# Two attention branches mixed by a gate, on one core: the same 1599 steps in another order

## The chip, the core and the metric

The kernel runs on one core of one Trainium2 chip. The metric is the time of one execution in microseconds of device time. Inside the core five engines run beside each other, each through a queue of its own: TensorE (PE in the profile, with its weight loads as PEld), VectorE (DVE), ScalarE (ACT), GpSimd (POOL) and SyncE (SP), which here only issues DMAs. Waits between engines and transfers are semaphores.

## The reference

One input `x` of 2048 tokens and 640 features goes through two attention branches of 32 heads with 20 features each; a sigmoid gate per token mixes the two outputs. Shapes are B=1, S=2048, D=640, H=32, Dh=20.

```python
def _A_ref(x, wqkv, w_phi, wo):                  # linear attention
    q, k, v = ...(x @ wqkv)...
    pq = einsum('bhsd,hdf->bhsf', q, w_phi);  pk = ... k, w_phi
    phi_q = concatenate([softmax(pq), softmax(-pq)], -1);  phi_k = ...
    kv = einsum('bhsf,bhsd->bhfd', phi_k, v);  z = einsum('bhsf->bhf', phi_k)
    num = einsum('bhqf,bhfd->bhqd', phi_q, kv)
    den = einsum('bhqf,bhf->bhq', phi_q, z)[..., None] + 1e-06
    return (num / den) ... @ wo

def _B_ref(x, wq, wk, wv, wo, beta):             # causal attention with a memory
    for s in range(4):                           # segments of 512 tokens
        p = softmax(qs ks^T * scale + causal mask);  a_dot = p vs
        pq = phi(qs);  a_mem = (pq M) / (pq z + 1e-06)      # phi(t) = t+1 or exp(t)
        o = sigmoid(beta) * a_mem + (1 - sigmoid(beta)) * a_dot
        pk = phi(ks);  M = M + pk^T vs;  z = z + sum(pk)
    return o ... @ wo

g = sigmoid((x * gate_w).sum(-1, keepdims=True))
return g * _A_ref(x, ...) + (1 - g) * _B_ref(x, ...)
```

## The kernel before

The tokens are cut into 16 chunks of 128 and 4 segments of 512, the heads into 8 groups of four. A function for every part of the computation takes an index and a step number; a step issues the instructions of one engine (or one DMA) for one piece of the work. One string, `ORDER`, lists all 1599 steps in the order in which they are issued. Its words are read by this loop:

```python
for word in "".join(ORDER).split():
    i = done.get(word[:2], 0)
    done[word[:2]] = i + 1
    at = word[2:]
    STEPS[word[0]](WHICH.get(word[:2], int)(i), int(word[1]), int(at) if at.isdigit() else None,
                   sca.copy if at == "a" else vec.tensor_copy)
```

A word is a letter (which function), a digit (which step) and, where there is one, a third character: a digit names the slot of PSUM that the step's tile takes, an `a` has the result copied out of PSUM by ScalarE instead of VectorE. The index is a count: the third `P0` in the list is score batch 2. All instructions go through the class `Kept`, which keeps them in program order, so each engine's queue has the list's order and no engine overtakes inside it. That is also why every instruction in the profile has line 117, the line of that class.

The steps, by letter:

- `T` turns the first 512 tokens on TensorE (`tp_ps`), `L` loads the other three segments turned. `w` are matmuls on zeros. `k`, `v`, `q` project keys, values and queries of the second branch (`proj`, `q_ps`); `K` makes key features, `k2` and `q2` bring keys and queries to the layout for the scores by DMA (`kTs`, `qTp`).
- `F` and `W` fold `w_phi` into the weights of the first branch (`fold_ps`); `D` loads the query weight turned. `A` makes that branch's key features (`k_ps`, two exponentials `Ek`, their sum, its reciprocal, the product `phk`), `B` its values and the gate's logits (`v_ps`, `vA`), `S` and `s` the sums `z`, `X` the products `KV`.
- `f` makes the first branch's query features for a segment: one matmul `pf_ps`, then two exponentials `ET` on ScalarE (`f1`, `f2`). `d` has the denominators, `n` the numerators: `n0` and `n1` matmuls (`num_ps`), `n2` and `n3` multiply on VectorE (`t`), `n4` adds on GpSimd (`oA`).
- `P` are the scores of the second branch, in 80 batches: `P0` writes row-tiled matmuls into `st_ps`, `P1` is one exponential of 128x2048 on ScalarE (`PT`), `P3` puts zeros above the diagonal on GpSimd. From batch 3 on, `st_ps` is one tile of four PSUM banks with one buffer (`banks4`).
- `U` has the attended values of a head group: `U0` column-tiled matmuls (`uv_ps`), `U1` a copy `uT`, `U2` a transposing DMA `uN`, `U3` a reciprocal on VectorE, `U4` and `U5` on GpSimd. The last four groups go through `V` instead, with no transposition (`nd_ps`).
- `Y` makes query features, `M` reads and updates the memory (`mem_ps`, `Mbd`). `l` turns finished rows by DMA (`oT`), `o` is the output projection (`o_ps`, a copy `osb`, a store). `R` loads the two output weights.
- The last four chunks of rows end in the tail: `t` turns the rows of the first branch in one DMA (into a tile that is named `phik`), `b` those of the second branch in three (into one named `kTs`); `p`, `a`, `e`, `z` are the products with the output weights, `h` copies and stores. `p0` of chunks 1 and 2 uses the four banks of the scores (`banks4("o2_ps")`).

The other four PSUM banks go by slot: a tile takes the slot that its word names, and the first write into it waits until the tile that was there has been read.

Of the kernel before, what the change touches and what calls it, by code (L numbers as in the profile page):

```python
# [15 lines left out]
def kernel(  # L16
# [800 lines left out]
    def tail_out(j, step, at, ev):  # L817
# [18 lines left out]


    ORDER = (
# [60 lines left out]

    done = {}  # L900
    for word in "".join(ORDER).split():
# [35 lines left out]
```

## Time and profile before

| what | us |
| --- | --- |
| three runs | 291.45, 291.5, 294.0 |
| median | 291.5 |
| profiled execution | 292.36 |
| its span in the profile | 290.6 |
| TensorE busy | 278.1 |
| VectorE busy | 239.8 |
| ScalarE busy | 239.6 |
| GpSimd busy | 183.8 |

The span runs from the first to the last instruction of the profiled execution; 292.36 − 290.6 = 1.8 us of its time lie outside. The granted clock of TensorE was 1.00. In a view of an engine's order of time, a line has start, duration, engine, line, operation, output and inputs by name, and in brackets the engine's idle time before it with what ended that. Durations of matmuls overlap the next one's, so a step's cost on TensorE is read from the distance of starts.

### The profile page before, as it was taken

The numbers are of one execution on the slowest core, as the hardware profiler recorded it, in microseconds if no ns is written. First come the engines' busy times: TensorE is split into PE (matmuls) and PEld (weight loads), VectorE is DVE, ScalarE is ACT, GpSimd is POOL, SyncE is SP. The second block draws the span as 40 slices with busy tenths as digits, with TensorE's granted clock in tenths as the row PEclk, the third lists the DMA queues.
The fourth block names the chain that finished last, engine by engine and source line by source line (L and its number), as shares of the span: only waits on it lengthen the run. The fifth ranks groups of instructions, "written<-read, shape, count | busy, mean of one in ns | idle before, by whom it ended". The sixth has DMA issues, their size and how long they took to land.

```text
span 290.6 us, 8207 instructions
## 1 busy us (share of the span) xinstructions
PE 278.1 (96%) x3233; PEld 176.2 (61%) x3233; DVE 239.8 (83%) x576; ACT 239.6 (82%) x260; POOL 183.8 (63%) x305
## 2 busy tenths in 40 slices
PE   8999999999999999999999999999999999898994
PEld 4676666667677546565546556556555555566673
DVE  5969999999699539999889988798898769989613
ACT  2478976998867899999999988999899998888801
POOL 8050000037346846797996899989789996998610
PEclk9999999999999999999999999999999999999999
DMA  7999960100110694546243425141736114356422
GB/s 226 252 237 215 166 142 11 36 2 20 20 20 20 203 158 89 72 86 134 39 92 72 106 58 104 39 106 36 124 72 139 26 41 111 83 122 126 106 62 90
DMA packets 79591, 28.10 MB, mean 97 GB/s; under 512 B 69952, under 2 KB 79552, under 8 KB 79552
## 3 DMA queue, kind: packets, MB, share of 16 engines
q1 hardware_dynamic: 78608, 26.84, 45.3%
q10 hardware_dynamic: 944, 0.74, 0.8%
q8 instruction: 25, 0.41, 0.6%
q14 instruction: 14, 0.11, 0.1%
HBM read 5.61 MB, written 2.62 MB: 28 GB/s over the span
## 4 chain that ended last, share of the span: by engine, by line
PE 66%; ACT 18%; DMA 5%; DVE 4%; POOL 3%; issue 3%; DVEq 0%; ACTq 0%; SPq 0%; POOLq 0%
ACT PT L117 15%; PE o_ps L117 9%; PE proj L117 8%; PE v_ps L117 8%; PE k_ps L117 8%; PE st_ps L117 7%; PE pf_ps L117 6%; PE q_ps L117 6%; PE uv_ps L117 4%; PE kv_ps L117 4%; DMA phk<-in_A_wqkv_dram 3%; PE mem_ps L117 2%; PE num_ps L117 2%; ACT ET L117 2%; PE zb_ps L117 1%
## 5 line engine op out<-in xcount | busy, mean ns | idle before, releaser
L117 ACT ACTIVATE PT<-st_ps 128x2048 bf16<-128x2048 f32 (+1 forms) x83 | 151.2, 1826 | 18.5 <-PE st_ps L117 14.0
L117 POOL TENSOR_SCALAR_AFFINE_SELECT PT<-PT 128x512 bf16<-128x512 bf16 (+2 forms) x116 | 80.5, 708 | 37.7 <-ACT PT L117 37.2
L117 PEld LDWEIGHTS <-xT 128*128 128x128 bf16 x640 | 59.5, 98 | 28.4 <-issue 5.7
L117 PE MATMUL st_ps<-qTp,kTs 32*128 32x384 bf16 (+3 forms) x512 | 31.8, 300 | 5.0 <-ACT PT L117 4.7
L117 ACT ACTIVATE Ek<-k_ps 128x640 bf16<-128x640 f32 x32 | 26.2, 893 | 6.2 <-PE k_ps L117 4.3
L117 POOL TENSOR_TENSOR Msb<-Msb,mtmp 128x84 f32<-128x84 f32 x24 | 9.3, 386 | 33.9 <-DVE mtmp L117 33.7
L117 DVE TENSOR_TENSOR t<-num_ps,dd 128x320 f32<-128x320 f32 x64 | 28.0, 481 | 2.3 <-POOL oA L117 1.3
L117 POOL TENSOR_TENSOR oA<-t,t 128x320 bf16<-128x320 f32 x32 | 29.1, 914 | 0.9 <-DVE t L117 0.7
L117 PEld LDWEIGHTS <-oT 128*128 128x128 bf16 x240 | 22.2, 98 | 10.4 <-issue 2.2
L117 PEld LDWEIGHTS <-kTs 32*128 32x128 bf16 (+1 forms) x552 | 14.8, 92 | 20.3 <-issue 16.3
L117 PE MATMUL proj<-WvB,xT 128*128 128x320 bf16 x160 | 26.2, 300 | 0.2 <-ACT vB L117 0.2
L117 PE MATMUL proj<-WkB,xT 128*128 128x320 bf16 x160 | 25.9, 300 | 0.0
L117 PE MATMUL q_ps<-xT,WqB 128*128 128x512 bf16 x100 | 24.9, 380 | 0.0
L117 PE MATMUL pf_ps<-xT,WqA 128*128 128x512 bf16 x100 | 24.9, 379 | 0.0
L117 PE MATMUL v_ps<-WvA,xT 128*128 128x320 bf16 (+1 forms) x160 | 24.5, 300 | 0.0
L117 PE MATMUL k_ps<-qTp,xT 128*128 128x320 bf16 x160 | 23.7, 299 | 0.1
L117 DVE TENSOR_REDUCE ksum<-Ek 128x64 f32<-128x1280 bf16 x16 | 23.3, 1455 | 0.0
L117 ACT ACTIVATE ET<-pf_ps 128x512 bf16<-128x512 f32 x40 | 22.0, 627 | 0.0
L117 POOL TENSOR_TENSOR oB<-td,tm 128x320 bf16<-128x320 f32 (+4 forms) x25 | 20.8, 835 | 0.4
L117 PE MATMUL o_ps<-WoA,oT 128*128 128x320 bf16 x120 | 20.3, 300 | 0.3 <-DVE tm L117 0.3
L117 PE MATMUL uv_ps<-PT,vB 128*32 128x512 bf16 (+1 forms) x448 | 20.4, 302 | 0.1
L117 PEld LDWEIGHTS <-phk 128*128 128x128 bf16 x370 | 17.6, 98 | 4.4 <-DMA phk<-in_A_x_dram 1.7
(115 smaller groups left out, 490.0 us busy)
## 6 DMA issues: line engine op xcount, KB each, us to landing
out_dram<-osb SPq DMA_DIRECT2D x12, 160.0 KB
qTp<-qd SPq DMA_DIRECT2D x8, 128.0 KB
WvB<-in_B_wv_dram SPq DMA_DIRECT2D x1, 800.0 KB
vA<-in_B_wq_dram SPq DMA_DIRECT2D x1, 800.0 KB
WvA<-in_A_wqkv_dram SPq DMA_DIRECT2D x1, 800.0 KB
WoA<-in_A_wo_dram SPq DMA_DIRECT2D x1, 800.0 KB
WoB<-in_B_wo_dram SPq DMA_DIRECT2D x1, 800.0 KB
qTp<-qd SPq DMA_DIRECT2D x8, 96.0 KB
```

The costliest lines, as they stand in the source:

```text
L117: return lambda *a, **k: kept(f(*a, **k))
```

## The change

Only the string `ORDER` is changed. The new list has the same 1599 words by letter, step and index; what differs is their order, the PSUM slots they name, and some of the `a` marks. Copies by ScalarE before and after are: `B` 23 and 22, `q` 8 and 7, `v` 4 and 5, `U` 3 and 4, `T` 0 and 1, `o` 8 and 4, `h` 2 and 4; `F` and `W` stay at 12. The first and the last lines of the diff:

```diff
-        "T00 w0 T1 T01 T02 T1 T1 T03 k00 T1 k01 k1 k02 I0 k03 k1 k00 k1 k1 K0 k01 K1 k1 K0 k02 K2 "
-        "K1 v03 k1 K2 K0 k00 k1 v1a K1 v01 k1 K2 F00 K0 L0 F01 K1 v1 v02 F1a K2 F2a v03 F1 F2 v1a "
-        "F00 v1 v00 F1a F2a F01 r0 r1 v1 v01 F1 D0 F00 F2 v02 r0 v1 F1a v03 F2a v1 r1 J4 A01 r0 "
...
-        "n10 o1 n2 P00 M02 n3 P1 n03 P3 n11 b0 M2 V00 n2 n3 M3 n4 V4 M4 Y0 Y1 P00 n4 o03 V1 P1 Y2 "
-        "P3 t0 V2 o1 Y0 V3 P3 P00 M01 Y1 P1 o02 M5 M2 Y2 o2 M3 P3 o1a P00 M4 M03 P1 V00 M2 M3 V4 "
-        "p02 V1 p11 V2 V3 P3 P00 o00 P1 M5 a0 M4 b0 o1a P3 V03 o2 V4 p00 V1 V2 V3 p01 M5 a0 b0 "
-        "p00 p13 e0 a0 e0 e0 z0 z1 z0 h0 z1 a0 h1 h0a h1 h2 h2 z0 z1 e0 h0 z0 h1 z1 h0 h2 h1a h2 ")
+        "T00 w0 T1 k01 T02 k1 T03 T1 T00 T1 k01 I1 I2 T1a I3 I4 k1 k02 I0 k03 k1 k00 k1 K0 k01 K1 "
+        "k1 K0 K2 k02 K1 k1 v03 K2 K0 v00 k1 K1 v1a v01 K2 v1a v02 v1 F00 v1 F01 L0 F1a v03 F1 "
+        "F2a F2 F00 v1 v00 F1a F2a F01 v1 F00 F1 v01 r0 F1a F2 F2a k02 r1 v1 D0 A01 r0 k1 K0 K1 "
...
+        "P3 n3 V3 n4 M4 Y0 Y1 P00 M5 o1 t0 o01 P1 Y2 P3 M02 o1 Y0 M2 P3 P00 Y1 p00 P1 p13 o2 M3 "
+        "V01 Y2 M4 V4 P3 V1 P00 V2 M02 P1 V3 a0 M2 M5 M3 p00 P3 b0 M4 V01 V4 a0 V1 V2 V3 M5 p01 "
+        "b0 e0 a0 p02 p11 z0 z1 e0 h0a h1 e0 z0 z1 h2 a0 h0a h1 h2 z0 z1 e0 h0a h1 z0 z1 h2 h0a "
+        "h1 h2 ")
```

In words: at the start, the first key projection stands between the turnings of `x`; before the first fold `F0` there are seven key and four value projections (`k0`, `v0`), where the old list has eight and two. Before the first score batch stand all 16 matmul steps of `A` and 24 of `B`, in the old list 14 and 18. In the middle the same kinds of steps are dealt out otherwise between the batches. In the tail, `p0` of chunk 1 follows the last score batch after `M0` and `a0` of chunk 0, where the old list has an output projection, `a0`, the last group's `V0` and `V4` before it.

107 rows, old and new, of the table ORDER are left out of this document.

## The prediction

> **What bounds the kernel now.** I read the page's head first, then the stretches between marks of the scores, then TensorE's own order of time, and last the waits.
>
> ```profile
> span 290.6 us, 8207 instructions
> PE 278.1 (96%) x3233; PEld 176.2 (61%) x3233; DVE 239.8 (83%) x576; ACT 239.6 (82%) x260; POOL 183.8 (63%) x305
> PE 66%; ACT 18%; DMA 5%; DVE 4%; POOL 3%; issue 3%; DVEq 0%; ACTq 0%; SPq 0%; POOLq 0%
> ```
>
> TensorE is busy 96% of the span and holds two thirds of the chain that ended last; ScalarE holds 18%. By the busy figure 290.6 − 278.1 = 12.5 us of room is left. The list keeps every engine's queue in the list's order, so the room can be found only between steps.
>
> ```profile
> 0.00:13.73 13.73, 11.96 (x79) 7.35 (x80) 10.16 (x23) 4.46 (x7) 6.40 (x21) 1.00 0.97 233
> 13.73:59.03 45.30, 45.17 (x358) 31.62 (x358) 42.23 (x74) 36.40 (x65) 5.39 (x7) 1.00 0.67 136
> 59.03:98.50 39.47, 39.43 (x592) 27.95 (x591) 33.03 (x95) 31.66 (x33) 20.92 (x33) 1.00 0.11 22
> 98.50:157.10 58.60, 56.92 (x670) 31.99 (x670) 48.75 (x118) 56.66 (x58) 46.32 (x78) 1.00 0.61 111
> 157.10:201.50 44.40, 43.95 (x528) 25.42 (x531) 38.58 (x99) 41.97 (x40) 39.32 (x68) 1.00 0.38 77
> 201.50:240.50 39.00, 37.84 (x434) 22.41 (x430) 31.92 (x86) 36.74 (x36) 34.76 (x56) 1.00 0.40 79
> 240.50:273.91 33.41, 29.88 (x462) 20.23 (x455) 30.32 (x74) 28.63 (x23) 27.91 (x40) 1.00 0.50 114
> 273.91:290.60 16.69, 12.93 (x133) 9.27 (x132) 4.82 (x12) 3.04 (x4) 2.83 (x5) 1.00 0.21 66
> ```
>
> The columns are the stretch, its length, then busy time of PE, PEld, DVE, ACT and POOL, and the granted clock, 1.00 throughout. The marks are the start of the first fold (13.73) and of score batches 0, 13, 34, 51, 66 and 79 of 80. TensorE is full until 98.50; from there idle time grows from stretch to stretch, and in the one from 240.50 it is 33.41 − 29.88 = 3.5 us. This is what that looks like:
>
> ```profile
> 266.65 0.40 PE L117 MATMUL st_ps<-qTp,kTs 32*128 32x384 bf16 x8 [0.45 <-ACT PT L117]
> 266.98 0.85 PE L117 MATMUL o_ps<-WoA,oT 128*128 128x320 bf16 x5
> 267.67 0.84 PE L117 MATMUL o_ps<-WoB,oT 128*128 128x320 bf16 x5
> 269.08 0.40 PE L117 MATMUL st_ps<-qTp,kTs 32*128 32x256 bf16 x8 [0.57 <-ACT PT L117]
> 271.46 0.40 PE L117 MATMUL st_ps<-qTp,kTs 32*128 32x512 bf16 x4 [0.36 <-ACT PT L117]
> ...
> 267.15 1.88 ACT L117 ACTIVATE PT<-st_ps 128x2048 bf16<-128x2048 f32 x1
> 269.53 1.88 ACT L117 ACTIVATE PT<-st_ps 128x2048 bf16<-128x2048 f32 x1
> 271.99 1.88 ACT L117 ACTIVATE PT<-st_ps 128x2048 bf16<-128x2048 f32 x1 [0.26 <-PE st_ps L117]
> ```
>
> From batch 3 on there is one tile of four banks for the scores. TensorE can write batch n+1 only when ScalarE has read batch n, and ScalarE starts only when TensorE has written: 266.65, 269.08, 271.46 are 2.43 and 2.38 apart, and so are the exponentials (2.38, 2.46). I take 2.43 us as the shortest step between two batches. Whatever the list gives TensorE between two batches below 2.43 us is lost; what it gives above costs its own time.
>
> **TensorE's time from a list.** Starts that follow without a wait give each step's cost: five matmuls of 320 columns take 267.67 − 266.98 = 0.69 us, a batch of scores 266.98 − 266.65 = 0.33. Before a row-tiled step, TensorE loses about 0.1 more:
>
> ```profile
> 113.57 0.84 PE L117 MATMUL proj<-WkB,xT 128*128 128x320 bf16 x5
> 114.38 0.40 PE L117 MATMUL st_ps<-qTp,kTs 32*128 32x512 bf16 x4
> ```
>
> The same five take 114.38 − 113.57 = 0.81 here. Read off in this way for every kind of step and summed over the list from batch to batch, with the missing part up to 2.43 added, the old list gives 39.05 + 0.42 = 39.47 for batches 0 to 13, 56.15 + 2.18 = 58.33 to 34, 43.45 + 0.96 = 44.41 to 51, 37.18 + 1.35 = 38.53 to 66 and 28.61 + 3.73 = 32.34 to 79. Measured are 39.47, 58.60, 44.40, 39.00, 33.41. The rule misses 1.7 us of 214.9, of which the largest piece is one bank:
>
> ```profile
> PE num_ps L117 <- DVE t L117: 1.2, 1, 1.2
> PE st_ps L117 <- ACT PT L117: 4.7, 16, 0.6
> DVE rden L117 <- DMA uN<-uT: 3.6, 2, 3.3
> PEld L117 <- issue: 40.4, 166, 1.3
> ```
>
> So the same sum over the new list should tell most of its time.
>
> **The change part by part.** It removes and adds no work: both lists hold 1599 words, the same steps with the same indices and 3228 matmuls besides the five warm ones. It moves steps, gives PSUM tiles to other banks, and changes which engine empties some tiles: above all, four output copies go from ScalarE to VectorE before the tail, and in the tail the four first halves of the last rows' copies go to ScalarE. Both lists make 86 changes into a row- or column-tiled step, so these cancel.
>
> *Work moved between stretches: 0.* The old list has 53.6 us of TensorE work before batch 0, 204.4 between batches 0 and 79 and 12.8 behind; the new one 59.4, 199.8 and 11.6. More keys and values of the linear branch run ahead of the first scores, where nothing ties TensorE to ScalarE. The three differences sum to zero.
>
> *Start: −0.7.*
>
> ```profile
> 3.32 0.71 PE L117 MATMUL tp_ps<-ident,phk 128*128 128x128 bf16 x5
> 13.73 0.81 PE L117 MATMUL fold_ps<-phk 128*128 128x140 bf16 x12 [0.51 <-DMA phk<-in_A_wqkv_dram]
> ...
> 4.51 9.18 DMA phk<-in_A_wqkv_dram
> ```
>
> The first fold needs a transposed weight that lands at 4.51 + 9.18 = 13.69. Ahead of it the old list has 8.80 us of TensorE work, the new one 9.48, since seven key and four value projections lie before it for eight and two. The landing does not move (same loads, same order), so 0.68 us of work go into a wait that is there anyway. If the wait were only the 0.51 shown, it would be −0.5.
>
> *Batches 0 to 13: −0.3.* Missing up to 2.43 us: 0.42 before, 0.12 after.
>
> *Batches 13 to 79: −1.5.* Intervals below 2.43: 30 before with 8.21 us missing, 26 after with 6.67. By stretch the missing time goes 2.18 to 0.99, 0.96 to 0.61, 1.35 to 2.06 and 3.73 to 3.01.
>
> *Two feature exponentials in one interval: +0.6.*
>
> ```profile
> 230.17 1.93 ACT L117 ACTIVATE PT<-st_ps 128x2048 bf16<-128x2048 f32 x1
> 231.93 1.16 ACT L117 ACTIVATE ET<-pf_ps 128x512 bf16<-128x512 f32 x2
> 232.88 1.97 ACT L117 ACTIVATE PT<-st_ps 128x2048 bf16<-128x2048 f32 x1
> ```
>
> With two of them ScalarE needs 232.88 − 230.17 = 2.71 us for an interval. The old list gives TensorE 2.68, 2.86, 2.56 and 2.76 (10.86) in the last four such intervals, 61 to 64, just what ScalarE needs (10.84). The new list gives 2.68, 2.48, 2.56, 2.76 (10.48), and its last interval carries a query exponential too, of some 0.5 us, ahead of an interval with 3.55 us of TensorE work that can absorb it. That is +0.4 to +0.9.
>
> *The tail: +0.4.*
>
> ```profile
> 274.42 1.88 ACT L117 ACTIVATE PT<-st_ps 128x2048 bf16<-128x2048 f32 x1 [0.56 <-PE st_ps L117]
> 277.99 1.79 PE L117 MATMUL o_ps<-WoB,kTs 128*128 128x320 bf16 x12
> 267.33 2.51 SPq L117 DMA_TRANSPOSE phik<-oA  x1
> ```
>
> The last rows' products for rows 1 and 2 reuse the score tile, so they need the last exponential, which ends at 274.42 + 1.88 = 276.30, 2.4 us after batch 79 started. The old list comes to them 4.1 us after it; the new one 1.9 us after it, and TensorE stands about 0.4. Behind the waiting products stand the last head group's products and all that follows, so the end moves as much. The transposition of the linear branch's last rows is used 4.3 us of listed work behind its word instead of 6.1; the time lost up to 2.43 us in the two batches between makes it 5.0. On SyncE it takes 2.51 us to issue and lands some time after. I take that as just in time: 0, with +1 as its upper end.
>
> *Smaller things: 0.* A PSUM bank is taken again less than 1.0 us of TensorE work after its last writer 17 times instead of 21; the three closest (0.31, 0.31, 0.47) become one (0.47), which may give back the wait of 1.2 us above. Against that, the attended values turned through a transposing DMA are read sooner behind their matmuls:
>
> ```profile
> 116.49 0.73 PE L117 MATMUL uv_ps<-PT,vB 128*32 128x512 bf16 x16
> 118.16 2.86 DMA uN<-uT
> ```
>
> That path took 118.16 + 2.86 − 116.49 = 4.53 us. In the list the shortest distance from matmul to read was 5.0; now it is 4.3, and 4.6 and 4.9 stand beside it. The 3.3 us that VectorE stood for one such transfer, behind the two output weights' loads, cost TensorE next to nothing, and the new list puts that transfer further behind these loads (10.2 us of listed work for 6.3). I set −1.2 and +1.2 as the ends and 0 in the middle.
>
> Sum: −0.7 − 0.3 − 1.5 + 0.6 + 0.4 = −1.5. The profiled execution took 292.36 us beside a span of 290.6, 0.9 above the median of 291.5, so the span would be 289.1, its execution 290.9, and the median 290.0.
>
> The Trainium skill says in "Perfetto Trace Analysis", section "Identifying the Most-Contended Engine", that the busy share of matmuls is a poor measure of the room left, since pipelined matmuls look smaller than they are, and that weight-load time should be used. Here the load row reads 61%, which would leave some 114 us of room; the spacing of starts leaves about 20 of the 290.6, since 262.6 us of listed work stand between the first transposition at 3.32 and the end. By that rule a reordering could bring far more than 1.5 us; the rows give no place where it could.
>
> **The rivals.**
>
> *VectorE becomes the bound: 292.9.* It has the four copies more. Its listed work by mean durations goes from 43.4 to 45.4 us for batches 34 to 51 and from 39.5 to 40.3 for 51 to 66, where I expect stretches of 43.9 and 38.9. If those sums could not overlap, the stretches would be 1.5 and 1.4 longer: 290.0 + 2.9. From the point where reads of turned values wait on VectorE as well (a path 1.2 us longer than 4.53, one more transposition's issue ahead on SyncE), with half of eight such waits reaching TensorE, 4 × 1.2 = 4.8 instead: 294.8. For it: 9 tenths in many slices. Against it: the window from 157.10 shows 38.58 us busy in 44.40 although the same sum says 43.4, so the instructions overlap.
>
> *The tail's transposition comes late: 292.* GpSimd is busy 27.91 of 33.41 us there, and the sums that feed the transposition queue behind its masks; two of them late is some 2 us on the end.
>
> *Collisions go away: 288.* The 1.7 us that the rule misses are single waits of the old order. If the new one, with wider bank distances, has none and its exponentials fit, 290.0 − 1.5 − 0.6 = 287.9.
>
> *The cap is what counts.* The densest 20 us hold 360 matmuls instead of 377, the densest 10 us 207 instead of 203, so the new list hardly does what its words say.
>
> ```profile
> q8 instruction: 25, 0.41, 0.6%
> ```
>
> Instruction fetch moves 25 packets of 16 KB in the whole span. If the 40.4 us that weight loads stand for "issue" were fetch, 17/377 of it would be 1.8 us, and the time 288.2. The Trainium skill, "Runtime: NRT & Kernel Launch", section "Instruction fetch mechanics", has fetches stream ahead and mostly hidden; the trace shows no TensorE stall beside one.
>
> **How the numbers follow.** The forecast (290.0, within 288.7 to 291.5) 0.45; VectorE 0.27, most of it at the upper price; the tail's transposition 0.10; collisions gone 0.13; the cap 0.05. About 1% is what a measurement of this kernel tells from no change: faster than 288.6 comes from the two faster cases and the forecast's edge, 0.20; slower than 294.4 from VectorE's upper price, 0.22; the rest 0.58. The range reaches from collisions gone to VectorE's upper price: 287.6 to 294.8.
>
> **What would show it.** Right: the first fold still at 13.7 but with more work before it; batch 0 near 64.1, batch 13 near 98.2 and batch 79 near 273.2; waits of scores for the exponential fewer and shorter; a wait of about 0.4 us in the products that reuse the score tile. Wrong: VectorE with 9s and TensorE waiting for copies or for t between batches 34 and 66; a wait for the transposed rows in the tail; batches 13 to 79 longer than 175.4 us, though the list gives less.

## The result

The changed kernel takes 294.77 us (median of 12 runs, 293.59 to 296.68), the kernel before 291.64 beside it (12 runs, 291.29 to 294.0): ratio 1.0096, 95% interval 1.0076 to 1.0117. It is slower by about 1% where a gain of 0.5% was forecast. One run below, the first with the fetches moved, has one execution at 293.69 us and five from 298.67 to 300.61, so its total is read only beside that of a later run with the same start.

The page's head and the chain of the profiled execution (293.68 us, span 292.0):

```profile
span 292.0 us, 8185 instructions
PE 277.3 (95%) x3213; PEld 175.8 (60%) x3233; DVE 239.5 (82%) x577; ACT 240.2 (82%) x259; POOL 182.8 (63%) x305
PE 57%; ACT 15%; POOL 9%; DMA 8%; DVE 6%; issue 4%; DVEq 0%; ACTq 0%; POOLq 0%
```

The busy times are those of before (20 of TensorE's matmul records are missing). What changed is the chain: GpSimd, DMA and VectorE held 3, 5 and 4% of it, now 9, 8 and 6%. The stretches between the same marks (first fold, score batches 0, 13, 34, 51, 66 and 79), in the columns used above (batches and transpositions are counted from 0):

```profile
13.64:63.76 50.12, 49.96 (x388) 35.14 (x390) 48.35 (x77) 41.74 (x72) 6.79 (x4) 1.00 0.59 122
63.76:98.16 34.40, 34.17 (x554) 24.38 (x556) 27.76 (x86) 27.66 (x26) 19.79 (x38) 1.00 0.12 23
98.16:156.51 58.35, 56.87 (x663) 31.42 (x670) 47.40 (x122) 55.08 (x57) 44.71 (x78) 1.00 0.55 103
156.51:203.40 46.89, 44.05 (x525) 25.21 (x521) 37.44 (x97) 42.66 (x39) 38.24 (x64) 1.00 0.45 86
203.40:243.59 40.19, 37.79 (x459) 22.43 (x461) 34.21 (x89) 36.47 (x34) 35.42 (x59) 1.00 0.34 74
243.59:275.84 32.25, 30.38 (x432) 20.91 (x429) 29.04 (x74) 28.15 (x22) 28.59 (x40) 1.00 0.62 123
275.84:292.00 16.16, 11.87 (x126) 8.42 (x125) 5.45 (x14) 3.56 (x5) 2.86 (x5) 0.99 0.19 58
```

The length less PE's busy time is TensorE's idle time by stretch: from batch 34 to 51 it is 46.89 − 44.05 = 2.8 us, before 44.40 − 43.95 = 0.45. Batches 13 to 79 take 177.7 us, before 175.4: the sign that the prediction had named for itself. The waits (us in total, times, longest) say what for:

```profile
DVE rden L117 <- DMA uN<-uT: 9.0, 9, 1.9
PE st_ps L117 <- ACT PT L117: 3.2, 10, 0.5
PE num_ps L117 <- DVE uT L117: 1.7, 2, 1.5
```

TensorE waits less for the exponentials (3.2 us, before 4.7), as the new list was to bring, and VectorE waits nine times instead of twice for a transposition of attended values. The worst place, by the orders of time of SyncE, VectorE and TensorE:

```profile
170.49 2.28 SPq L117 DMA_DIRECT2D qTp<-qd  x3
172.89 1.22 SPq L117 DMA_TRANSPOSE uN<-uT  x1
...
177.38 0.25 DVE L117 RECIPROCAL rden<-uN 128x16 f32<-128x16 bf16 x1 [1.92 <-DMA uN<-uT]
177.55 0.63 DVE L117 CAST uT<-uv_ps 128x512 bf16<-128x512 f32 x1
178.95 0.48 DVE L117 TENSOR_TENSOR tm<-mem_ps,rdm 128x320 f32<-128x320 f32 x1
...
178.23 0.32 PE L117 MATMUL num_ps<-KV,ET 128*128 128x80 bf16 x3 [1.50 <-DVE uT L117]
179.47 0.84 PE L117 MATMUL proj<-WvB,xT 128*128 128x320 bf16 x5 [0.60 <-DVE tm L117]
```

Transposition 14 is issued at 172.89, behind the query stores, and lands at 177.36. VectorE stands for it for 1.92 us, the copies queued behind it come late, and TensorE waits 1.50 and 0.60 us for their banks. Between batches 41 and 43 the rule of 2.43 us gives 4.86; measured are 7.04. Not every such wait costs something: VectorE stands 1.91 us for number 16 as well, and TensorE has no wait longer than 0.15 us from 183 to 198.

**Why it lands so late.** From the chain of waits, the flights of transpositions 14 and 21 (start, duration), and from the DMA view of just these two flights and of one that met nothing (191.13 to 193.57), the queues with packets, MB and share of the time of 16 engines. A flight is the time from a transposition's issue to its landing; q1 carries the data, q8 the packets of 16 KB:

```profile
172.89 4.47 DMA uN<-uT
217.46 4.08 DMA uN<-uT
...
q1 hardware_dynamic: 1259, 0.39, 71.9%
q8 instruction: 1, 0.02, 2.0%
q14 instruction: 1, 0.01, 1.2%
...
q1 hardware_dynamic: 551, 0.13, 17.1%
q8 instruction: 1, 0.02, 1.5%
...
q1 hardware_dynamic: 544, 0.13, 27.8%
```

Into each of the two falls one fetch of 16 KB of TensorE's instructions (at 174.1 and 219.5); number 14 shares its flight with query stores besides (0.39 MB for 0.13) and with a smaller packet of another instruction queue, q14. The undisturbed flight has no instruction row, and took 2.43 us. Over all flights of the trace much the same holds: with no instruction packet and nothing else in the queue they take 2.40 to 2.43 us, and with a fetch just before them or in their first 2.1 us 2.8 to 4.5. Other data lengthen a flight too: numbers 5, 8 and 12, with no packet of 16 KB, take 3.25, 2.90 and 2.98 us, and number 4 of the kernel before, behind the weight loads, took 5.88 without one. Over the fourteen profiles of this document, 82 flights that met neither a fetch nor other data took 2.40 to 2.48 us, and 22 that met only a fetch, begun in their first 2.1 us, 2.70 to 4.38. A landing is reported in sixteen parts: of number 21's, fifteen come 2.38 to 2.48 us after the issue and one at 4.08, so it is one part that is late; of number 14's all come at 3.98 to 4.47. The fetches come about every 128 matmuls with their weight loads (25 for some 3230 of each), so they meet mostly the same transpositions in every execution, give or take a microsecond.

### The profile page after: what moved, and what is told of

It reads as the page before. It is cut to its first block, busy times and chain, and to the rows that moved or that the text cites. A ratio compares the mean times of both kernels' runs of the same rounds, so it can differ in the third digit from the quotient of the medians.

```text
span 292.0 us, 8185 instructions
## 1 busy us (share of the span) xinstructions
PE 277.3 (95%) x3213; PEld 175.8 (60%) x3233; DVE 239.5 (82%) x577; ACT 240.2 (82%) x259; POOL 182.8 (63%) x305
## 4 chain that ended last, share of the span: by engine, by line
PE 57%; ACT 15%; POOL 9%; DMA 8%; DVE 6%; issue 4%; DVEq 0%; ACTq 0%; POOLq 0%
ACT PT L117 12%; PE proj L117 9%; PE v_ps L117 8%; PE k_ps L117 7%; PE o_ps L117 7%; DMA uN<-uT 6%; PE st_ps L117 5%; PE q_ps L117 4%; PE kv_ps L117 4%; POOL PT L117 4%; PE uv_ps L117 3%; PE pf_ps L117 3%; PE num_ps L117 3%; POOL oA L117 2%; ACT ET L117 2%
## 5 line engine op out<-in xcount | busy, mean ns | idle before, releaser
L117 POOL TENSOR_SCALAR_AFFINE_SELECT PT<-PT 128x512 bf16<-128x512 bf16 (+2 forms) x116 | 79.7, 700 | 28.9 <-ACT PT L117 28.8
L117 ACT ACTIVATE Ek<-k_ps 128x640 bf16<-128x640 f32 x32 | 26.8, 900 | 5.4 <-issue 1.6
L117 POOL TENSOR_TENSOR oA<-t,t 128x320 bf16<-128x320 f32 x32 | 28.4, 890 | 3.4 <-DVE t L117 3.3
L117 POOL MEMSET qTp<- 128x4096 bf16 x1 | 3.5, 3512 | 40.3 <-ACT vA L117 40.3
L117 PE MATMUL pf_ps<-xT,WqA 128*128 128x512 bf16 x89 | 24.0, 380 | 1.4 <-DVE t L117 0.6
L117 PE MATMUL q_ps<-xT,WqB 128*128 128x512 bf16 x91 | 24.1, 379 | 0.5
L117 POOL TENSOR_TENSOR oB<-td,tm 128x320 bf16<-128x320 f32 (+4 forms) x25 | 20.2, 812 | 2.1 <-DVE td L117 0.6
L117 PEld LDWEIGHTS <-ET 128*128 128x128 bf16 x352 | 16.2, 97 | 7.1 <-issue 5.2
```

What stands on the lines that cost most here:

```text
L117: return lambda *a, **k: kept(f(*a, **k))
```

## The experiments

Three theories. A: fetches hit transpositions, and the new list's reads stand too close behind to take it. B: only the place of number 14 behind the query stores matters. C: VectorE is full, by its work and the copies it was given.

**The same kernel again.**

> The changed kernel once more, for a second profile and its time beside the next three. Theory A (instruction fetch): where a 16 KB fetch of TensorE's instructions falls into the flight of a transposing DMA of the attended values, that DMA lands some 4 us after its issue instead of 2.4, VectorE waits, and TensorE behind it. The fetches come at fixed places in TensorE's instruction count, so the same transfers should be late as in the first profile: numbers 14, 16, 18 and 21, with 3 to 4.5 us each. Theory B (queue and list): the late transfer is number 14, because its issue stands behind three query stores on SyncE; the rest is chance, and other transfers may be late this time. Theory C (VectorE): the four copies that went to VectorE and its recips fill it, and waits for transfers are no cause. All three: about 294.8 us.

295.06 us beside 292.0 (1.0106, 1.007 to 1.0141). Numbers 14, 16, 18 and 21 are late again, with 4.36, 4.07, 2.83 and 4.20 us, and number 6, which took 2.49 in the first profile, takes 3.70: its fetch had come at the end of the flight and now falls into its middle. That speaks for A, and it may be one reason why executions of this kernel lie 3 us apart; batch 20, just behind it, takes 0.4 us longer here.

**Fetches moved, list untouched** (three runs). Edit of the first and, with 60 and 80 for 40 and 128, of the other two:

```diff
-    warm_up(WARM, 4)
+    for i in range(40):
+        ten.matmul(wu[:, 0, 0:128], lhsT=wz, rhs=wz[:, 0:128], start=True, stop=True)
```

> The changed kernel with its first five matmuls on zeros (512 columns each) made into 40 of 128 columns: about the same time ahead of the first transposition, the same list, but TensorE's instruction count is 35 matmuls higher from there on, so each fetch comes about a quarter of a block, 3 us, earlier against the list. Theory A: transfers 14, 16, 18 and 21 land 2.4 to 3 us after issue, VectorE's waits for them fall from 9 us to under 5, and the time falls by 1.5 to 3 us, to about 292.3; others (11, 12, 19) may be hit instead and take back part. Theory B and theory C: nothing in the list has moved, so the time stays within 0.4 us of the changed kernel's.

Numbers 14, 16, 18 and 21 take 2.91, 2.40, 2.99 and 2.40 us, as A has it, and batches 39 to 44 take 12.99 us instead of 14.51. But numbers 2, 4, 19, 20, 24 and 27 are hit (4.33, 6.33, 3.44, 4.26, 3.25 and 3.93), VectorE's waits grow to 11.5 us, and the 40 small matmuls end 2 us later than the five did, which shifts the whole start (batch 0 comes 1.9 us later). The expected gain, to 292.3 us, did not come: the median is 299.05, near the 299.47 of the run below with the same start. Part of it may be the clock and not the fetches: in the profiled execution the granted clock was 0.50 for 3.4 us from 116.2 and again from 225.5.

> The kernel before with its first five matmuls on zeros made into 60 of 80 columns: the list is the same, TensorE's instruction count is 55 matmuls higher, so the fetches come some 5 us earlier against the list and fall, by the trace of before, into the flights of transfers 1, 4, 5, 7, 12, 22, 24 and 25 instead of 3, 6, 16 and 18. Theory A: slower by 0.5 to 2 us, about 293. Theories B and C: no change, within 0.4 us of 291.6.

293.95 beside 292.0 (1.0063, 1.0044 to 1.0081), a little over A's 293 and inside its 0.5 to 2 us: the kernel before, with no word moved and a start 0.2 us later, loses 2 us. Numbers 5, 7 and 17 take 3.78, 4.49 and 4.41. Number 17 was not on the list of the expectation, nor was number 2 (4.00), and numbers 12, 22 and 25, which were, take 2.43 to 2.50. Number 17, by SyncE's and VectorE's order of time and the DMA view of its flight:

```profile
191.47 1.20 SPq L117 DMA_TRANSPOSE uN<-uT  x1
195.90 0.25 DVE L117 RECIPROCAL rden<-uN 128x16 f32<-128x16 bf16 x1 [1.58 <-DMA uN<-uT]
...
q8 instruction: 1, 0.02, 2.0%
```

That wait costs TensorE nothing: batches 34 to 51 take 44.35 us with it and without. What the profiled execution loses lies elsewhere: 1.2 us at batches 18, 20 and 22, 0.65 at 51 and 52, and 0.2 in the start. The first of these follow number 5, by VectorE's and TensorE's order of time:

```profile
115.74 0.25 DVE L117 RECIPROCAL rden<-uN 128x16 f32<-128x16 bf16 x1 [0.84 <-POOL PT L117]
...
116.39 0.84 PE L117 MATMUL proj<-WvB,xT 128*128 128x320 bf16 x5 [0.30 <-DVE kpads L117]
119.37 0.84 PE L117 MATMUL proj<-WkB,xT 128*128 128x320 bf16 x5 [0.37 <-DVE uT L117]
```

Number 5 lands at 115.64, and the reciprocal starts 0.1 us later. The view names a mask of GpSimd that ends at 115.70, but in the trace of before the reciprocal started at 114.74 while that mask still ran. Beside the 0.65 us no late transposition stands. B and C expected no change, and have no room for this one; of its 2 us, A accounts for 1.2.

> The changed kernel with the first five matmuls on zeros made into 60 of 80 columns, which moved the start of the kernel before by only 0.2 us (40 of 128 columns moved it by 2). The list is untouched; the fetches come 55 matmuls earlier against it. Theory A: transfers 14, 16 and 21 land 2.4 to 3 us after issue and what TensorE loses in batches 41 and 42 falls from 2.2 to under 0.8 us, in 58 and 59 from 1.1 to under 0.6; transfers 2, 7, 17, 20 and 22 are hit instead and lose there what they lack in distance. The total is not told by this, 293 to 297. Theories B and C: batches 41, 42, 58 and 59 lose what they lost, since no word has moved.

297.24 beside 291.97 (1.0159, 1.0128 to 1.0189). Numbers 14, 16 and 21 take 2.92, 2.40 and 2.40 us. Number 14 is issued behind the same three stores, yet VectorE's wait for it is 0.61 instead of 1.92, and the wait of 1.50 us on TensorE is gone; that of 0.60 stays:

```profile
174.51 2.29 SPq L117 DMA_DIRECT2D qTp<-qd  x3
176.92 1.22 SPq L117 DMA_TRANSPOSE uN<-uT  x1
...
179.86 0.25 DVE L117 RECIPROCAL rden<-uN 128x16 f32<-128x16 bf16 x1 [0.61 <-DMA uN<-uT]
...
181.96 0.84 PE L117 MATMUL proj<-WvB,xT 128*128 128x320 bf16 x5 [0.60 <-DVE tm L117]
```

Batches 41 and 42 lose 0.9 us instead of 2.2 (0.8 was the bound), 58 and 59 0.1 instead of 1.1. The start is 1.8 us later here too, though in the list before it was 0.2; I had not expected that, and it takes the total 0.2 over the range. With each set against its own runs of the kernel before, it is 2.1 us over the changed kernel, so the fetches in sum cost some 0.3. What was won at those places was lost where the fetches now fall: number 22, with 4.03 us in flight, holds VectorE for 1.75, and numbers 1, 5 and 15, which had not been expected, take 4.38, 4.69 and 4.43.

**Number 14 issued first.**

```diff
 ... k02 U1
+U2
 P1 q2 Y2 o00 P3 q2 k1 P3
-U2
 P00 o1 ...
```

> The changed kernel with one word moved: the issue of transposition 14 of the attended values stands right behind its copy, ahead of the two query stores it followed. Theory A: it is issued near 171 and lands near 173.4, ahead of the fetch at 174.1, and the 2.1 us of TensorE waits in batches 41 and 42 go: about 292.7 us. Theory B: the same 2.1 us go, for the queue's sake. Theory C: VectorE is full anyway, less than 0.5 us goes.

292.93 beside 292.0 (1.0018, 0.9998 to 1.0038), 2.1 us less than the changed kernel in the same comparison: the number that A and B gave, and C did not. Batches 39 to 44 take 12.33 us. It leaves most of VectorE's waits (9.6 us), for other transpositions, and by itself does not separate A from B.

**Reads later in the changed kernel, reads earlier in the one before.**

One of the 17 reads of the first run, and one of the second:

```diff
-... M01 n4 U3 v03 v1 M6 Y2 U4 U00 M6 M7 ...
+... M01 n4 v03 v1 M6 Y2 U00 U3 U4 M6 M7 ...

-... M03 P1 q02 k00 ... P3 P00 U3 k03 P1 ...
+... M03 P1 U3 q02 k00 ... P3 P00 k03 P1 ...
```

> The changed kernel with transposition 14 issued right behind its copy, and with every read U3 that stands less than 6.0 us of listed TensorE work behind its U0 moved down the list to at least 6.0 (17 of 28 reads, by 0.4 to 2 us); nothing else. Theory A (a transfer that is hit by an instruction fetch lands up to 1.7 us late, and reads that stand only 4.3 to 5.6 us behind cannot take that): VectorE's waits for these transfers fall from 9 to 10 us to under 3, TensorE's waits for VectorE in batches 39 to 44, 44 to 51 and 57 to 61 mostly go, 2.5 to 3.5 us in all: 291 to 292. Theory B (one queue order at number 14): no better than the run with number 14 alone, 292.9. Theory C (VectorE is full by its work, with the copies it was given): 294 or more; the waits for transfers go, but others take their place.

292.99 beside 292.02 (1.003, 1.0011 to 1.0049). VectorE's waits for the transpositions fall to 2.5 us, batches 57 to 61 take 10.35 us instead of 11.16, but the time is no better than with number 14 alone: the steps behind a read on GpSimd (U4, U5) went down with it, and between batches 33 and 34 TensorE waits 1.2 us for a mask that GpSimd now does later. A's size was wrong here (291 to 292 was expected): later for all is not free.

> The kernel before with every read U3 moved up the list until it stands at most 5.0 us of listed TensorE work behind its U0 (before: 5.0 to 7.6; now 3.7 to 5.0); nothing else. Theory A: VectorE waits for most of the 28 transfers, 10 to 20 us in all, and TensorE loses 2 to 4 us: 294 to 296. Theory B: no change, 292. Theory C: VectorE's work is the same, so at most 0.5 us.

296.89 beside 292.02 (1.0162, 1.0132 to 1.0192): 4.9 us slower, more than A's 2 to 4, by nothing but earlier reads. The profiled execution, the fastest of the six (295.73), has ten waits of VectorE for transpositions, 8.9 us, so fewer than I expected, and TensorE's largest losses at batches 18 (1.3 us), 43 and 48 (0.6 and 1.0). Of the ten only number 16 had a fetch well inside its flight, so this run shows what a short distance costs and not what a fetch does.

**The copies back to ScalarE.**

In words, since the edit is the mark of eight `o1` steps (one string, cut):

```diff
-o1a for 0, 7, 13, 21
+o1a for 1, 7, 8, 13, 14, 19, 22, 23
```

> The changed kernel with the output copies marked for ScalarE as in the kernel before: eight of them (1, 7, 8, 13, 14, 19, 22, 23) instead of four (0, 7, 13, 21). Theory C: VectorE has some 1.9 us of work less where it is full, and 1 to 2.5 us come back: 292.5 to 294. Theories A and B: the waits for transfers stay, and ScalarE, which sets the pace of the scores, has the copies between its exponentials: 294.5 to 296.

294.88 beside 292.02 (1.0103, 1.0072 to 1.0133), the changed kernel's time. Four copies on VectorE cost nothing that is seen, though this run alone can't exclude that ScalarE lost as much by taking them. C falls by the last runs below, which leave the four copies on VectorE and take 291.6 and 291.43. By chance the fetch at number 21 starts 2.26 us after the issue here, not 2.08: its flight takes 2.40 us, and batches 58 and 59 take 4.92 instead of 5.92, though the nearest mark that changed stands behind batch 54.

**The tail.**

```diff
-... M5 M3 p00 P3 b0 M4 V01 V4 a0 ...
+... M5 M3 P3 b0 M4 V01 V4 p00 a0 ...
```

> The run with the reads later, and in the tail the products of the last rows that reuse the score tile (p0 of row 1) moved behind the last head group's products, so that the last exponential is read before they come. The wait of 0.4 us that the prediction put there should go: 0.4 us less than the run with the reads later alone, under all three theories; by theory A 290.6 to 291.6, which would be the fastest so far.

293.89 beside 292.02 (1.0064, 1.0039 to 1.0089): 0.9 us more than without the move, where 0.4 less was expected. The tail takes 16.75 us instead of 16.11. The wait stood in the changed kernel as the prediction had it, but in TensorE's order of time it has moved to the products that came forward, and one for a mask has joined it. The first line is the changed kernel's, the two others this run's:

```profile
278.27 0.97 PE L117 MATMUL o_ps<-WoB,kTs 128*128 128x320 bf16 x6 [0.42 <-ACT PT L117]
...
277.38 0.92 PE L117 MATMUL nd_ps<-vB,PT 128*128 128x32 bf16 x25 [0.38 <-ACT PT L117]
278.68 0.49 PE L117 MATMUL nd_ps<-vB,PT 128*128 128x32 bf16 x13 [0.37 <-POOL PT L117]
```

**Only the places that lose.** Number 15 is put right behind its copy as well, reads 6, 16 and 21 go down the list:

```diff
-... n4 k1 U3 k2 Y0 ...  n10 v02 n2 l0 ...
+... n4 k1 k2 Y0 ...  n10 v02 U3 n2 l0 ...
```

> The changed kernel with words moved at five places where its traces show a wait: transpositions 14 and 15 issued right behind their copies, the reads 6, 16 and 21 moved to 6.0 us or more of listed work behind their matmuls, and one exponential of key features (K0 and K1 number 6) behind the exponential of score batch 17. Nothing else. Theory A: the waits come to 2.2 us (14), 1.0 (21), 0.3 to 1.1 (15, 16), 0.3 to 1 (6) and 0.5 (batch 17), 4 to 4.5 us in all; 290.5 to 291.3, which is below the kernel before and about what the prediction had for the changed one without these waits. Theory B: 292.9, as with number 14 alone. Theory C: not below 293.

291.6 beside 292.15 (0.998, 0.9962 to 0.9998): just clear of the kernel before, and some 3.6 us under the changed one when each is set against its own runs of the kernel before, but 0.3 us short of A's range. The fifth place was a mistake: the exponential moved behind batch 17 came late for VectorE, and TensorE waited 1.26 us one batch later.

> The run with the five places, and the first five matmuls on zeros made into 40 of 128 columns, so that the fetches come a quarter of a block earlier against the list. Theory A: transfers 2, 4, 19, 20, 24 and 27 are hit now; of these, 2, 19 and 24 have short distances (4.3 to 5.4 us), and 1 to 3 us are lost against the run without: 291.5 to 294. Theories B and C: the list is the same, no change.

299.47 beside 292.15 (1.0249, 1.0209 to 1.0288). The direction is A's, the size is not: 7.9 us. Some 2 are the later start, as in the first of these runs. Transpositions 2, 4, 7, 19 and 20 have 4.38, 6.20, 4.13, 3.62 and 4.19 us in flight, and batches 0 to 13 took 1.6, 16 to 18 1.7 and 56 and 57 2.3 us longer. The 1.7 are not the fetch's alone: TensorE waits 1.5 us behind number 4, but the granted clock is 0.50 from 115.7 to 119.1 as well, and five matmuls of 512 columns take 2.34 us there for 1.24. By an estimate from these figures, this list is some 4 to 5 us better or worse by where the fetches fall.

The last run takes that fifth place back and moves the last segment's token gates:

```diff
-... P00 G0 P3 n03 G1 P1 n10 n02 n2 n11 o2 G2 n3 f03 U2 n2 n4 n3 G3 P00 P3 O0 ...
+... P00 P3 n03 P1 n10 n02 n2 n11 o2 n3 f03 U2 n2 n4 n3 P00 P3 ... o1 f2 G0 ... f1 G1 G2 G3 O0 ...
```

> The run with the five places, but the exponential of key features left where the changed kernel has it (in that run its move made batch 18 wait 1.3 us and saved 0.5 in batch 17), and the last segment's token gates (G and O number 3, four small VectorE steps) moved from batches 59 and 60 to 60 and 61, since they stand between the products t whose bank TensorE waits for (0.6 us). Theory A: 0.6 and 0.6 us less than the run with the five places, 290.2 to 290.8, some 1.5 us below the kernel before: what the prediction had for the changed kernel. Theory B and theory C: no better than 291.6.

291.43 beside 291.97 (0.9974, 0.9959 to 0.999), the fastest list here, yet 0.6 us over the expected range. In the profiles batches 13 to 79 are 1.1 us shorter than with the five places, about the 1.2 expected, but batch 0 comes 0.85 us later (64.45 for 63.60). The stretches from batch 34 on:

```profile
157.27:201.88 44.61, 43.66 (x525) 25.13 (x521) 37.15 (x97) 42.60 (x39) 38.38 (x65) 1.00 0.46 91
201.88:241.20 39.32, 37.73 (x460) 22.57 (x462) 35.11 (x89) 36.50 (x34) 35.25 (x59) 1.00 0.34 75
241.20:273.44 32.24, 30.35 (x432) 20.86 (x430) 29.06 (x74) 28.09 (x21) 28.51 (x40) 1.00 0.62 123
```

With the waits taken out, batches 13 to 79 take 174.6 us, 0.8 less than before.

## Why the prediction was wrong

**Start: right in size, but it trades.** Batch 0 was put at 64.1 us; over the eight profiles with this start it came between 63.60 and 64.67. TensorE no longer waits at the first fold, as its order of time shows:

```profile
13.58 0.79 PE L117 MATMUL fold_ps<-phk 128*128 128x140 bf16 x12
```

But the wait had also been a cushion. Where the first loads land later, as in the run with number 14 first, the first fold starts 0.9 us later and batch 0 with it. The 60 small matmuls show the same: in both lists they put TensorE's first transposition at 5.04 us (3.32 before, 3.55 in the new list). The old list had 10.4 us from there to the first fold for 8.80 of work, and batch 0 came 0.2 later; the new one had no such idle time, and batch 0 came 1.8 later.

**Batches 0 to 13 and 66 to 79: right.** The prediction's rule, summed over the new list, gave 34.15 and 32.21 us, measured are 34.40 and 32.25. The 1.2 us that one bank had cost in the last stretch are gone, and with them 1.1 us, as the bank distances suggested.

**Batches 13 to 66: the step that failed.** The rule gave 57.44, 43.94 and 38.89 us, measured are 58.35, 46.89 and 40.19: 5.2 us over (the old list: 0.7). The double exponentials, put at 0.6, cost 0.4. The failing term is the one called "smaller things: 0". It saw that the read of a transposition stands 4.3 to 5.6 us behind its matmuls instead of 5.0 and more, and set it against a path of 4.53 us with an end of +1.2. The two places that it should have held cost 2.2 (number 14) and 1.1 us (number 21), 3.3 in all. Batches 16, 17 and 34 cost another 1.2, which no run ties to a transposition: 0.5 of it, at batch 17, went when an exponential of key features was moved. The term's error was the price of a transfer: one flight was taken for all, while the traces show 2.4 us alone and up to 4.5 with a fetch or a store beside it. What a late one costs TensorE goes by the copies of PSUM tiles that stand behind it in VectorE's queue: 2.2 us for VectorE's 1.92 (number 14), 1.1 for 1.25 (number 21), nothing for 1.91 (number 16). The wait of 3.3 us in the trace of before, which cost next to nothing, was taken for the rule, and it is none.

**The rivals.** VectorE as the bound was priced at 292.9 by work and at 294.8 from the point where its reads wait. The first falls with the copies put back (no change) and with the repaired lists, which have VectorE's work and take 291.4 to 291.6. The second is near what happened, since reads that wait on VectorE held TensorE, but in two places instead of four, for 3.3 us instead of 4.8, and by fetches instead of one more issue on SyncE. That its 294.8 meets the measured 294.77 is luck. The tail's transposition did not come late: TensorE's one wait behind batch 79 is the 0.42 us for the exponential. Collisions went in the last stretch and came back in the middle ones. The rival called the cap, where instruction fetch counts, was held to be nothing, since TensorE stands for no fetch. That is so here as well; the fetch did its harm to a transposing DMA that the step did not look at. The Trainium skill says in "Runtime: NRT & Kernel Launch", section "Instruction fetch mechanics", that crossing a block of 16 KiB is mostly hidden. For TensorE the traces agree; a transposing DMA in flight they show up to 2.1 us longer (4.47 for 2.4).

**The tail: right** in its wait (0.42 for 0.4), wrong in the thought that only the products' place made it: the other order waits too. By its own figures the tail should have become 0.8 us shorter (12.8 to 11.6 of work, plus 0.4); it went from 16.69 to 16.16.

**The base.** The sum was made against one execution, 0.7 us slower than the median of 291.64, and some of what it took off may not be lost in a usual one. The repaired list, which has the predicted stretches, is 0.54 us better by medians, where the sum had 1.5. Two figures of the working are off without changing a term: the rule misses 1.8 us of 214.9, not 1.7, and 262.6 us of work from 3.32 on leave 24.7 of the 290.6, not about 20.

What stays open: the 0.65 us at batches 51 and 52 of the kernel before with its fetches moved, the 0.7 us of batches 16 and 34, and how much of the spread of the changed kernel's executions is the fetches and how much the first loads.

## What to carry to other kernels

In an engine's queue with an order by hand, a read of a transfer is a wait for all that stands behind it: give it the distance of a disturbed transfer, not of the median one, and only there, since moving all of them moves other engines' steps too. When a list is compared by summing one engine's work, the sum tells the stretches that this engine sets to within some tenths; what decides is then the margins that the sum does not hold. Before judging a list by its time, move the instruction fetches against it once: a time that changes by microseconds, beyond what the later start explains, says that luck is part of it.

## What the hardware showed unexpectedly

A 16 KB fetch of TensorE's instructions, whose one packet takes 0.9 to 1.5 us, lengthens a small transposing DMA from 2.4 to more than 4 us, even where data fill only 17% of the DMA engines' time (number 21). There, one of the sixteen parts of the landing came 1.6 us behind the others. Fetches sit at nearly fixed places of TensorE's instruction count, so mostly the same transfers are hit in each execution; 0.2 us can decide (number 21 with the copies put back). 55 more tiny matmuls at the start of a kernel, which compute nothing, changed the time of the kernel before by 2.0 us, 0.2 of it the start, and that of the changed one by 2.1, 1.8 of it the start.
